# Two changes to the scan pairs of a fused SSD and MLP kernel: B and C turned by VectorE in pairs 2 to 4, and the half form in pairs 4 and 5

## The chip, the core and the metric

The kernel runs on one core of a Trainium2 chip. TensorE is called PE, VectorE DVE, ScalarE ACT, GpSimd POOL; SP only issues DMAs. The time is that of one execution on the device, in microseconds, and the figure of a kernel is the median of its runs. The profile is that of one execution more, with its own span from first to last instruction.

## What is computed

The reference takes a Mamba-2 scan in chunks and puts its result through a two-layer MLP. For batch 4, 8 heads, 768 tokens, head size 32 and state size 16:

```python
log_a = np.log(np.clip(a, 1e-06, 1.0))
# for each chunk c of 32 tokens
cum = np.cumsum(la, axis=-1)
L = np.exp(cum[:, :, :, None] - cum[:, :, None, :]) * causal
M = np.einsum('bhin,bhjn->bhij', Cc, Bc) * L
y = np.einsum('bhij,bhjd->bhid', M, xc) + einsum(Cc, state) * exp(cum)
state = exp(sum(la)) * state + sum_j Bx_j * exp(cum[-1] - cum_j)
# then, over 3072 tokens of width 256
h = x @ w_in                                  # 256 x 2048, float64 weights
g = np.maximum(h, 0) + alpha * np.minimum(h, 0)
out = g @ w_out                               # 2048 x 256
```

The chunk length is free, since the scan gives the same result for any.

## The kernel before

**Pairs and groups.** The 3072 tokens are cut into 24 chunks of 128. Two chunks make a pair (12 pairs, 3 for each batch), two pairs a group of 512 tokens (6 groups). A pair of the scan leaves its result, transposed, in xT, and a group's xT is the moving operand of the MLP. Pairs 0 and 1 are made by `first_two` (L821) in chunks of 64. Pairs 2 and 3 make up group 1 and are run while group 0 goes through the plain MLP, pairs 4 and 5 (group 2) while group 1 goes through the MLP in a form of seven products instead of eight (`quad`, L1229), and so on.

**A pair (`pair`, L581)** is a generator, and `ssm(gp)` takes it one stage further. For pairs 4 and up ("fine") the stages are: the products B'x into a state (L629, or L618 in the half form), the new state (L642, DVE) and its masked copy (L645, POOL); the decays, as four scans over rows of `a` (`scan_half`, L554: DVE reads `abc` and a pattern of ones, `ident_p`, from PSUM); the spread C (`cz`, L679, ACT) and decayed C (`cd`, L682, POOL); the gram products of B and C (L742, or L731 in the half form); their product with the decays (L753, DVE); and the output products (L797 and L805, or L779 and L787), copied to xT by ACT (L817 or L815).

**The half form** applies from pair HALF = 6. A chunk of 128 is then held as two blocks of 64 tokens in the upper and the lower half of the partitions, one chunk in each half. Of the 128 x 128 decay matrix of a head only the causal 128 + 64 columns of the two blocks are made (SQ = 192 columns for the two chunks of a head, in place of 256), so that scans take 192 columns for a head, the gram products 128 and 64. It needs B and x loaded in blocks of 64 tokens (`load_tokens`, L139), rows of `a` with the last 64 columns repeated (`scratch["z", 1]`, written by `rows_out`, L472), the decay products in a matching order (`prt[1]`, L512), a changed lower half of `ident_p` (`halve_identity`, L421), and shifted copies of the decayed C and of the state (`moved`, L685, two ACT and two POOL copies).

**B and C.** Each pair has B by tokens (`nat[:, 0]`, rows of 64 bytes), for the state products. For the gram products B and C are wanted by channels (`bc`). Pairs 2, 3 and 4 load C in the same way (`load_bc`, L188), turn both with four PE transposes (L669) and copy the result from PSUM with ACT (L672). Pairs 5 and up (`turned`) load B and C a second time in rows of 512 bytes, eight tokens to a row (L213 to L217, four DMAs), and DVE turns them in blocks of 32 x 32 (`turn_bc`, L571).

**Weights.** w_in and w_out come as 64-bit floats in 16 pieces of 512 KB and are turned into 32-bit ones by ACT (L273, L283 or L286), POOL (L278), DVE (L296, L308) and POOL (L330). Up to six pieces are in flight.

**What sets the order.** Each engine runs the instructions in the order in which the program lists them, and waits where one needs a result of another; the order is written out by hand. In the loop over f = 4 to 15 (L1454) a step is `hidden(0, f)` on PE, a stage of pair 2 (f up to 10) and of pair 3 (from f = 9), some conversions, and `output(f - 4)`. `load_pair(3)` is issued at f = 5, `load_pair(4)` at f = 10, `bns[3]` and `bns[4]` (L521, POOL) at f = 8 and f = 14. After the loop come the token sums of group 1 (`token_sums`, L1176, POOL) and four stages of pair 4. Then `after(j)` (L1509) places the stages of later pairs between the products of a quad. All loads but a few at the start are issued by SP, in program order, and SP holds an issue back until the eighth DMA before it has landed.

Of the kernel before, what the change touches and what calls it, by code (L numbers as in the profile page):

```python
# [9 lines left out]
F32 = mybir.dt.float32  # L10
# [12 lines left out]
def kernel(  # L23
# [25 lines left out]
    nc = tc.nc  # L49
# [5 lines left out]
    N = B.shape[-1]  # L55
# [21 lines left out]
    WQ = 256  # L77
    HQ = Q // 2
    SQ = Q + HQ
    HALF = NP // 2  # L80
    assert H * N == P and HD == d_model and KC == 2 and R == CPB == 6
    assert NCH % GC == 0 and GT == 512 and NF % 8 == 0 and d_model <= WQ

# [65 lines left out]
    def load_spread(gp, b, c):  # L149

        for w, t in enumerate(loads["p", gp][1] if gp >= HALF else ()):
            rows = scratch["z", b // 2].rearrange("(b h c) t -> b c h t", b=2, h=H)
            for k in range(2):
                nc.sync.dma_start(
                    out=t[HQ * k : HQ * (k + 1), : 4 * SQ].rearrange("p (h t) -> p h t", h=4),
                    in_=rows[b % 2, c + k, 4 * w : 4 * w + 4].unsqueeze(0)
                    .to_broadcast([HQ, 4, SQ]))
        for k, t in enumerate(loads["p", gp][1] if gp < HALF else ()):
            rows = scratch["z", b // 2].rearrange("(b h c) t -> b c h t", b=2, h=H)[b % 2, c + k]
            nc.sync.dma_start(out=t.rearrange("p (h t) -> p h t", h=H),  # L160
                              in_=rows.unsqueeze(0).to_broadcast([P, H, Q]))
            yield
# [7 lines left out]
    def load_pair(gp, decays=True, parted=False):  # L170


        b, c = divmod(2 * gp, CPB)
        turned = gp > GC
        nat = ldx.tile([P, 3, 2, H * N], F32, name="nat")
        xt = ldx.tile([P, 2, HD], F32, name="xt")

        ap = ldx.tile([P, 2 * Q], F32, name="ap")
        if gp == 0:
            load_a(ap, b, c)  # L180
        elif gp > NB:
            load_products(gp, ap)
        if gp == 0:
            load_rows(0, nc.scalar)
        abc = []
        if gp >= HALF:
            load_tokens(nat[:, 0], B[b], c * Q)
        def load_bc(k):  # L188
            ts = slice((c + k) * Q, (c + k + 1) * Q)
            for i, src in enumerate((B,) if turned else (B, C)):  # L190
                eng = nc.scalar if gp == 0 and i else nc.sync
                eng.dma_start(out=nat[:, i, k].rearrange("p (h n) -> p h n", h=H),  # L192
                              in_=src[b, :, ts, :].rearrange("h p n -> p h n"))

        def load_x(k):
            ts = slice((c + k) * Q, (c + k + 1) * Q)
            nc.sync.dma_start(out=xt[:, k].rearrange("p (h d) -> p h d", h=H),  # L197
                              in_=x[b, :, ts, :].rearrange("h p d -> p h d"))

        for k in range((1 if parted else 2) if gp < HALF else 0):  # L200
            load_bc(k)
            if gp >= NB:
                load_x(k)
        for k in range(2 if gp < NB else 0):
            load_x(k)
        if gp == 0:
            nc.scalar.dma_start(out=al_n, in_=moe_alpha.rearrange("(k p) -> k p", p=P))
            loads["a", 1] = prep.tile([P, 2 * Q], F32, name="a1")
            load_a(loads["a", 1], b, c + 2)
        for i, src in enumerate((B, C) if turned else ()):  # L210


            for e in range(2):  # L213
                first = src[b, e : e + 1, c * Q : (c + 2) * Q, :]
                nc.sync.dma_start(out=nat[:, 1 + e, i],
                                  in_=bass.AP(tensor=first.tensor, offset=first.offset,
                                              ap=[[2 * S * N, P // 32], [8 * N, 32], [1, 8 * N]]))  # L217
        for k in range(2 if gp >= NB else 0):
            abc.append(lda.tile([P, H * Q], F32, name="abc"))
        loads["p", gp] = nat, abc, xt, ap  # L220
        if gp >= HALF:
            load_tokens(xt, x[b], c * Q)
        if decays:
            for part in load_spread(gp, b, c):
                pass
        return lambda: load_bc(1), lambda: load_x(1)

    def load_second():

# [190 lines left out]

    def halve_identity():  # L421

        for s in range(2):
            nc.scalar.copy(
                out=ident_p[0][HQ:].rearrange("p (a s t) -> p s a t", a=2, s=2)[:, s],
                in_=ident[HQ:, HQ * (1 - s) : HQ * (2 - s)].unsqueeze(1).to_broadcast([HQ, 2, HQ]))
# [45 lines left out]
    def rows_out(i):  # L472


        if i == 0:
            scratch["z", 0] = dr.tile([RW, Q], F32, name="z0")
            nc.sync.dma_start(out=scratch["z", 0], in_=held.pop("z"))
            return
        d0 = held.pop(i)[:, :SQ]
        rpf = prep.tile([RW, Q], F32, name="rpf")  # L480
        nc.vector.tensor_tensor_scan(out=rpf, data0=d0[:, :Q], data1=zeros[:RW], initial=1.0,
                                     op0=ALU.mult, op1=ALU.add)
        nc.vector.memset(d0[:, :1], 0.0)
        for key, t in (("z", d0), ("pf", rpf)):
            scratch[key, i] = dr.tile([RW, t.shape[1]], F32, name=f"{key}{i}")
            nc.sync.dma_start(out=scratch[key, i], in_=t)

    def rows_short(r):

# [31 lines left out]
    def pair_loads(gp):  # L521

        b, c = divmod(2 * gp, CPB)
        nat, abc, xt, ap = loads["p", gp]

        bn = work.tile([P, 2, H * N], F32, name="bn")
        i, bi = divmod(b, 2)
        if gp >= HALF:
            pj = prt[i].rearrange("p (j b m h) -> p j b m h", j=2, b=2, h=H)[:, :, bi, c // 2]
        else:  # L530
            pj = (prt[i if gp >= NB else "short"]
                  .rearrange("p (b h c) -> p b c h", b=2, h=H)[:, bi, c : c + 2])
        nc.gpsimd.tensor_tensor(
            out=bn.rearrange("p k (h n) -> p k h n", h=H),
            in0=nat[:, 0].rearrange("p k (h n) -> p k h n", h=H),
            in1=pj.unsqueeze(3).to_broadcast([P, 2, H, N]), op=ALU.mult)
        return bn
# [16 lines left out]
    def scan_half(dec, abc, k, w):  # L554
# [10 lines left out]
        for i in range(2):  # L565
# [2 lines left out]
                                         data1=ident_p[0], initial=0.0, op0=ALU.mult,  # L568
                                         op1=ALU.add)

    def turn_bc(gp):  # L571

        bcs[gp] = work.tile([P, 4, Q], F32, name="bc")
        nc.vector.transpose(
            bcs[gp].rearrange("p (i k) t -> p i (k t)", i=2)
            .rearrange("p i (c b) -> p i b c", b=8),
            loads["p", gp][0][:, 1:].rearrange("p e i (b n) -> p (i b) e n", n=N))
        decs[gp] = work.tile([P, 2, H, Q], F32, name="dec")
        scan_half(decs[gp], loads["p", gp][1], 0, 0)

    def pair(gp):  # L581
# [24 lines left out]

        shifted = one.tile([P, 2, P], F32, name="shifted") if half else None

        def added_halves(banks):


            dps = [t[:, : 4 * D].rearrange("p (k m) -> p k m", k=2) for t in banks]
            for j in range(2):
                for r in range(4):
                    rs, hs = slice(32 * r, 32 * r + 32), slice(2 * r * D, 2 * (r + 1) * D)
                    for k in range(nk):
                        ks = slice(HQ * k, HQ * (k + 1))
                        nc.tensor.matmul(dps[k][rs, k], bn[ks, j, rs], xt[ks, j, hs],  # L618
                                         start=False, stop=j == 1,
                                         tile_position=(HQ * k, 32 * r),  # L620
                                         skip_group_check=True)
            return dps
# [30 lines left out]
        if fine:  # L653
            bn = bns.pop(gp) if gp in bns else pair_loads(gp)
            if half:
                dps = added_halves(beside.pop(gp))
            else:
                dps = added(beside.pop(gp) if gp in beside else ss_tile()[:, : 2 * Q])
            yield
# [3 lines left out]

        bc = bcs.pop(gp, None)
        if bc is None:
            tp = ss_tile()
            for i in range(2):
                for k in range(2):
                    nc.tensor.transpose(tp[:, (2 * i + k) * P : (2 * i + k + 1) * P],  # L669
                                        nat[:, i, k], ident)  # L670
            bc = work.tile([P, 4, Q], F32, name="bc")
            nc.scalar.copy(out=bc.rearrange("p i t -> p (i t)"), in_=tp)  # L672
        bh, ct = bc[:, :2], bc[:, 2:].rearrange("p k t -> p (k t)")
        cz = czp.tile([P, 2, 2, Q], F32, name="cz")
        cd = work.tile([P, 2, Q], F32, name="cd")
# [78 lines left out]
            if i == 1:  # L754
                yield
        if fine and gp + 1 < NP:
            if gp + 1 == HALF:
                halve_identity()
                halved.append(True)
            turn_bc(gp + 1)  # L760
        yield

# [691 lines left out]
    for f in range(FIRST, NF):  # L1454
# [5 lines left out]
        for part in range(2):  # L1460
# [5 lines left out]
            for i in CONVERTED.get((f, part), ()):  # L1466
                if isinstance(i, str):
                    convert_a(*pieces[int(i)])
                else:
                    convert_next(first=False)  # L1470
        if f == 14:
            bns[4] = pair_loads(4)
            rows_clamp(1)
# [1 line left out]
            rows_out(1)  # L1475
        if f == 8:
            bns[3] = pair_loads(3)
        output(f - FIRST)
        if f in in_steps:
            weight_sums(wi, in_sums, 0, in_steps[f])  # L1480
    early[0] = None
    beside[GC] = m5_bank[0][:, : 2 * Q]
    token_sums(1)
    ssm(2 * GC // 2, 4)

# [94 lines left out]
```

## Time and profile before

| | us |
|---|---|
| median of 3 runs (356.65 to 358.07) | 356.97 |
| profiled execution: span from first to last instruction | 355.9 |
| PE busy | 349.3 |
| DVE busy | 235.8 |
| POOL busy | 204.4 |
| ACT busy | 171.8 |

The views give no other time of the profiled execution than its span. A line of a timeline has the start in us from the beginning of the span, the length in us, the engine, the line of the code, the operation, what it writes and reads, the shape and the count; in brackets stands how long the engine was idle before it and what ended that. Matmuls are pipelined, so that the length of a PE group overlaps the next one; the distance from one start to the next is what a group takes of PE. In the chain, a line is start, length and what held the end up at that time.

### The profile page before, as it was taken

The page shows a single profiled execution, that of the slowest core. Times are in us where ns is not written, and L with a number is a line of the kernel's source. Part 1 is how long each engine was busy: PE and PEld are TensorE (multiplying, and loading weights), DVE is VectorE, ACT ScalarE, POOL GpSimd, SP SyncE. Part 2 cuts the span into 40 slices and gives each one's busy share as a digit, 9 for nine tenths or more (in the row PEclk, how much of TensorE's full clock was granted, in tenths as well). Part 3 has the DMA queues.
Part 4 walks back from the last instruction along what each step waited for, and adds up shares of the span by engine and source line. Part 5 has one row for each costly group of instructions (what it writes and reads, how often), then busy time and mean ns, then how long its engine had stood idle before and what let it go on. Part 6 is the DMA issues. An engine that isn't in the chain of part 4 may idle for free.

```text
span 355.9 us, 7778 instructions
## 1 busy us (share of the span) xinstructions
PE 349.3 (98%) x2985; PEld 284.4 (80%) x2985; DVE 235.8 (66%) x482; ACT 171.8 (48%) x391; POOL 204.4 (57%) x228
## 2 busy tenths in 40 slices
PE   8899999999999999999999999999999999999996
PEld 4576665578788888888888888888888888888885
DVE  6876986998748756847747856757856633643363
ACT  3477576535355346345345445345445344443431
POOL 6776568589939855725646626637526535434520
PEclk9999999999999999999999999999999999999999
DMA  7899989607345403503423423422001001001102
GB/s 138 182 202 270 329 174 279 148 17 159 106 83 128 102 3 75 104 2 77 78 57 74 86 51 71 85 55 65 11 2 31 0 2 29 2 1 31 31 0 59
DMA packets 105581, 30.24 MB, mean 85 GB/s; under 512 B 79896, under 2 KB 101448, under 8 KB 105544
## 3 DMA queue, kind: packets, MB, share of 16 engines
q1 hardware_dynamic: 103048, 29.43, 36.3%
q10 hardware_dynamic: 2496, 0.32, 0.6%
q8 instruction: 23, 0.38, 0.5%
q14 instruction: 14, 0.11, 0.1%
HBM read 26.32 MB, written 3.42 MB: 84 GB/s over the span
## 4 chain that ended last, share of the span: by engine, by line
PE 89%; SPq 4%; DMA 3%; DVE 2%; ACT 1%; POOL 1%; issue 0%; DVEq 0%; ACTq 0%
PE bank L1216 33%; PE hp L1241 29%; PE bank L1142 6%; PE ss L1241 6%; PE hp L1095 3%; DMA raw<-in_moe_w_in_dram 2%; SPq L192 2%; PE ss L787 1%; PE ss L731 1%; PE hp L1110 1%; PE bank L1209 1%; PE ss L805 1%; PE ss L779 1%; DMA xt<-in_x_dram 1%; SPq L197 1%; PE ss L742 1%
## 5 line engine op out<-in xcount | busy, mean ns | idle before, releaser
L1298 POOL TENSOR_TENSOR gt<-gt 128x512 f32<-128x512 f32 x58 | 74.2, 1279 | 21.1 <-DVE gt L1226 16.3
L1216 PE MATMUL bank<-gt,w_out 128*128 128x256 f32 x320 | 83.5, 381 | 0.0
L1216 PEld LDWEIGHTS bank<-gt,w_out 128*128 128x128 f32 x320 | 60.1, 190 | 9.2 <-issue 1.0
L1288 POOL TENSOR_TENSOR gt<-gt 128x512 f32<-128x512 f32 x20 | 25.4, 1269 | 62.5 <-DVE gt L1226 49.7
L1226 DVE SCALAR_TENSOR_TENSOR gt<-hp,s_mul,gt 128x256 f32<-128x256 f32 x96 | 42.0, 479 | 29.1 <-ACT gt L1224 26.8
L1224 ACT ACTIVATE gt<-hp,s_alpha 128x256 f32<-128x256 f32 x96 | 40.3, 471 | 34.5 <-PE hp L1241 31.4
L1216 PE MATMUL bank<-gt,ws 128*128 128x256 f32 x224 | 55.9, 379 | 0.0
L1216 PEld LDWEIGHTS bank<-gt,ws 128*128 128x128 f32 x224 | 42.3, 190 | 5.6
L1241 PE MATMUL hp<-xs,w_in 128*128 128x256 f32 x160 | 41.9, 384 | 0.0
L1241 PE MATMUL hp<-xs,ws 128*128 128x256 f32 x160 | 41.1, 380 | 0.0
L1267 DVE TENSOR_TENSOR hp<-hp,u 128x512 f32<-128x512 f32 x20 | 14.0, 700 | 35.2 <-ACT u L1265 35.2
L1241 PEld LDWEIGHTS hp<-xs,ws 128*128 128x128 f32 x160 | 30.3, 190 | 4.3 <-POOL xs L1183 0.2
L1241 PEld LDWEIGHTS hp<-xs,w_in 128*128 128x128 f32 x160 | 29.7, 190 | 4.5
L1142 PE MATMUL bank<-w_out,gt 128*128 128x256 f32 x128 | 31.1, 385 | 0.4 <-POOL w_out L330 0.4
L1142 PEld LDWEIGHTS bank<-w_out,gt 128*128 128x128 f32 x128 | 23.6, 190 | 7.2 <-issue 2.9
L1241 PE MATMUL ss<-xT,w_in 128*128 128x256 f32 x96 | 24.6, 379 | 0.0
L645 POOL TENSOR_TENSOR sm<-state,bmask 128x256 f32<-128x256 f32 (+1 forms) x10 | 6.2, 620 | 29.0 <-DVE state L642 29.0
L1095 PE MATMUL hp<-xT,w_in 128*128 128x512 f32 x48 | 22.8, 596 | 0.0
L561 DVE TENSOR_TENSOR_SCAN dec<-abc,bank 128x192 f32<-128x192 f32 x48 | 22.7, 522 | 0.0
L1256 ACT COPY m<-hp 128x512 f32<-128x512 f32 x8 | 4.7, 586 | 35.7 <-PE hp L1241 35.7
L1265 ACT COPY u<-hp 128x512 f32<-128x512 f32 x20 | 11.7, 585 | 19.4 <-PE hp L1241 19.4
L1226 DVE SCALAR_TENSOR_TENSOR gt<-c,s_mul,gt 128x256 f32<-128x256 f32 x40 | 20.6, 555 | 0.0
(232 smaller groups left out, 608.2 us busy)
## 6 DMA issues: line engine op xcount, KB each, us to landing
abc<-z SPq DMA_DIRECT2D x24, 192.0 KB
raw<-in_moe_w_in_dram SPq DMA_DIRECT2D x8, 512.0 KB
raw<-in_moe_w_out_dram SPq DMA_DIRECT2D x8, 512.0 KB
abc<-z SPq DMA_DIRECT2D x8, 512.0 KB
out_dram<-o_sb SPq DMA_DIRECT2D x32, 64.0 KB
nat<-in_B_dram SPq DMA_DIRECT2D x26, 64.0 KB
xt<-in_x_dram SPq DMA_DIRECT2D x12, 128.0 KB
xt<-in_x_dram SPq DMA_DIRECT2D x24, 64.0 KB
```

Of the source, the lines that this page charges most:

```text
L192: eng.dma_start(out=nat[:, i, k].rearrange("p (h n) -> p h n", h=H), in_=src[b, :, ts, :].rearrange("h p n -> p h n"))
L561: nc.vector.tensor_tensor_scan(out=dv[:, o : o + SQ], data0=abc[k][:, s : s + SQ], data1=ident_p[0][:, :SQ], initial=0.0, op0=ALU.mult, op ...
L1095: nc.tensor.matmul(hp, w_in[:, k, f * P : (f + 1) * P], xts[g][:, k], start=(k == 0), stop=(k == KC - 1))
L1142: nc.tensor.matmul(pos[0][t // 2][:, t % 2], gt[:, t * Q : (t + 1) * Q], w_out[:, f], start=(f == 0 and t % 2 == 0), stop=(f == NF - 1), s ...
L1216: nc.tensor.matmul(ms[g][i][:, h], w, blocks[g, z][n][:, p], start=(q == 0 and h == 0), stop=(q == NQ - 1), skip_group_check=True)
L1224: nc.scalar.mul(o[:, p], h[:, p], s_alpha[:, fs[p]])
L1226: nc.vector.scalar_tensor_tensor(out=o[:, p], in0=h[:, p], scalar=s_mul[:, fs[p]], in1=o[:, p], op0=ALU.mult, op1=ALU.max)
L1241: nc.tensor.matmul(to[:, p], w(2 * z + p), b, start=start and p == 0, stop=True, skip_group_check=True)
L1265: nc.scalar.copy(out=u2, in_=A)
L1267: nc.vector.tensor_tensor(out=Y, in0=Y, in1=u2, op=ALU.add)
L1288: nc.gpsimd.tensor_tensor(out=tc_, in0=g22, in1=g12, op=ALU.subtract)
L1298: eng.tensor_tensor(out=o, in0=x0, in1=x1, op=ALU.subtract)
```

## The change

`turned` now holds from pair 2 on and HALF is 4 in place of 6.

Pairs 2, 3 and 4 no longer load C in rows of 64 bytes; they load B and C a second time in rows of 512 bytes. For pair 2, whose loads are issued in two parts, the four new DMAs are issued with the second part. DVE turns the blocks: for pair 2 and pair 4 at the stage in which PE turned them before, for pair 3 at f = 8, ahead of its first stage. The PE transposes and the ACT copy are gone.

Pairs 4 and 5 take the half form. For that the rows of batches 0 and 1 are written once more with their last 64 columns repeated (`rows_repeated`, POOL and one DMA, at f = 6), the decay products are copied into the order of the half form (`rows_halved`, four ACT copies, at f = 12), and the lower half of `ident_p` is changed at f = 13 in place of the last stage of pair 5. Pair 4's state products go into two banks in place of one, and the first of them starts the accumulation there.

```diff
-    HALF = NP // 2
+    HALF = GC
...
-            rows = scratch["z", b // 2].rearrange("(b h c) t -> b c h t", b=2, h=H)
+            rows = scratch["zs", b // 2].rearrange("(b h c) t -> b c h t", b=2, h=H)
...
-        turned = gp > GC
+        turned = gp >= NB
...
-        for i, src in enumerate((B, C) if turned else ()):
-            for e in range(2):
-                first = src[b, e : e + 1, c * Q : (c + 2) * Q, :]
-                nc.sync.dma_start(out=nat[:, 1 + e, i], in_=bass.AP(...))
+        def load_blocks():
+            for i, src in enumerate((B, C)):
+                for e in range(2):
+                    first = src[b, e : e + 1, c * Q : (c + 2) * Q, :]
+                    nc.sync.dma_start(out=nat[:, 1 + e, i], in_=bass.AP(...))
+        if turned and not parted:
+            load_blocks()
...
-        return lambda: load_bc(1), lambda: load_x(1)
+        return lambda: (load_bc(1), load_blocks()), lambda: load_x(1)
...
     def halve_identity():
+        halved.append(True)
...
+    def rows_repeated():
+        d0 = held.pop(0)
+        nc.gpsimd.tensor_copy(out=d0[:, Q + 1 :], in_=d0[:, HQ + 1 : Q])
+        nc.gpsimd.memset(d0[:, :1], 0.0)
+        scratch["zs", 0] = dr.tile([RW, SQ], F32, name="zs0")
+        nc.sync.dma_start(out=scratch["zs", 0], in_=d0)
+
+    def rows_halved():
+        t = prep.tile([P, RW], F32, name="prth")
+        for v in range(2):
+            for j in range(2):
+                nc.scalar.copy(out=t[HQ * v : HQ * (v + 1)]..., in_=prt[0][HQ * j : HQ * (j + 1)]...)
+        prt["halves"] = t
...
+    def turned_bc(gp):
+        bc = work.tile([P, 4, Q], F32, name="bc")
+        nc.vector.transpose(bc..., loads["p", gp][0][:, 1:].rearrange("p e i (b n) -> p (i b) e n", n=N))
+        return bc
...
-                dps = added_halves(beside.pop(gp))
+                dps = added_halves(beside.pop(gp), gp == HALF)
...
         if bc is None:
-            tp = ss_tile()
-            for i in range(2):
-                for k in range(2):
-                    nc.tensor.transpose(tp[:, (2 * i + k) * P : (2 * i + k + 1) * P],
-                                        nat[:, i, k], ident)
-            bc = work.tile([P, 4, Q], F32, name="bc")
-            nc.scalar.copy(out=bc.rearrange("p i t -> p (i t)"), in_=tp)
+            bc = turned_bc(gp)
...
         if fine and gp + 1 < NP:
-            if gp + 1 == HALF:
-                halve_identity()
-                halved.append(True)
             turn_bc(gp + 1)
...
+        if f == 6:
+            rows_repeated()
+        if f == 12:
+            rows_halved()
+        if f == 13:
+            halve_identity()
...
         if f == 8:
             bns[3] = pair_loads(3)
+            bcs[3] = turned_bc(3)
...
-    beside[GC] = m5_bank[0][:, : 2 * Q]
+    beside[GC] = [m5_bank[0][:, : 2 * Q], ss_tile()[:, 2 * Q :]]
```

More of the change, by code (lines that the diff above doesn't have):

```diff
@@ L209, in load_pair @@
             load_a(loads["a", 1], b, c + 2)
-        for i, src in enumerate((B, C) if turned else ()):
-            for e in range(2):
-                first = src[b, e : e + 1, c * Q : (c + 2) * Q, :]
-                nc.sync.dma_start(out=nat[:, 1 + e, i],
-                                  in_=bass.AP(tensor=first.tensor, offset=first.offset,
-                                              ap=[[2 * S * N, P // 32], [8 * N, 32], [1, 8 * N]]))
+        def load_blocks():
+            for i, src in enumerate((B, C)):
+                for e in range(2):
+                    first = src[b, e : e + 1, c * Q : (c + 2) * Q, :]
+                    nc.sync.dma_start(out=nat[:, 1 + e, i],
+                                      in_=bass.AP(tensor=first.tensor, offset=first.offset,
+                                                  ap=[[2 * S * N, P // 32], [8 * N, 32], [1, 8 * N]]))
+        if turned and not parted:
+            load_blocks()
         for k in range(2 if gp >= NB else 0):
@@ L483, in rows_out @@
         nc.vector.memset(d0[:, :1], 0.0)
-        for key, t in (("z", d0), ("pf", rpf)):
+        for key, t in (("zs", d0), ("pf", rpf)):
             scratch[key, i] = dr.tile([RW, t.shape[1]], F32, name=f"{key}{i}")
             nc.sync.dma_start(out=scratch[key, i], in_=t)
+    def rows_repeated():
[8 more added lines that the diff above has]
+            for j in range(2):
+                nc.scalar.copy(
+                    out=t[HQ * v : HQ * (v + 1)]
+                    .rearrange("p (j b m h) -> p j b m h", j=2, b=2, h=H)[:, j],
+                    in_=prt[0][HQ * j : HQ * (j + 1)]
+                    .rearrange("p (b h m k) -> p k b m h", b=2, h=H, k=2)[:, v])
+        prt["halves"] = t
     def rows_short(r):
@@ L528, in pair_loads @@
         if gp >= HALF:
-            pj = prt[i].rearrange("p (j b m h) -> p j b m h", j=2, b=2, h=H)[:, :, bi, c // 2]
+            pj = prt[i if i else "halves"].rearrange(
+                "p (j b m h) -> p j b m h", j=2, b=2, h=H)[:, :, bi, c // 2]
         else:
@@ L569, in scan_half, with turn_bc @@
                                          op1=ALU.add)
-    def turn_bc(gp):
-        bcs[gp] = work.tile([P, 4, Q], F32, name="bc")
+    def turned_bc(gp):
+        bc = work.tile([P, 4, Q], F32, name="bc")
         nc.vector.transpose(
-            bcs[gp].rearrange("p (i k) t -> p i (k t)", i=2)
+            bc.rearrange("p (i k) t -> p i (k t)", i=2)
             .rearrange("p i (c b) -> p i b c", b=8),
             loads["p", gp][0][:, 1:].rearrange("p e i (b n) -> p (i b) e n", n=N))
+        return bc
+    def turn_bc(gp):
+        bcs[gp] = turned_bc(gp)
         decs[gp] = work.tile([P, 2, H, Q], F32, name="dec")
@@ L607, in pair, with added_halves @@
         shifted = one.tile([P, 2, P], F32, name="shifted") if half else None
-        def added_halves(banks):
+        def added_halves(banks, fresh=False):
             dps = [t[:, : 4 * D].rearrange("p (k m) -> p k m", k=2) for t in banks]
@@ L618, in added_halves @@
                         nc.tensor.matmul(dps[k][rs, k], bn[ks, j, rs], xt[ks, j, hs],
-                                         start=False, stop=j == 1,
+                                         start=fresh and j == 0, stop=j == 1,
                                          tile_position=(HQ * k, 32 * r),
```

## The prediction, made before the result was known

> **What bounds the kernel now.** I read the busy shares first, then the chain that ended last, then that chain in order of time, and last the timelines of single engines.
>
> ```profile
> PE 349.3 (98%) x2985; PEld 284.4 (80%) x2985; DVE 235.8 (66%) x482; ACT 171.8 (48%) x391; POOL 204.4 (57%) x228
> ...
> PE 89%; SPq 4%; DMA 3%; DVE 2%; ACT 1%; POOL 1%; issue 0%; DVEq 0%; ACTq 0%
> ```
>
> PE is busy in 98% of the span and holds 89% of the chain, at the full granted clock. So time can only come off by taking work from PE, and only where nothing else is due at the same moment. The second point needs the chain in order of time. These are its pieces from 29.8 us (start, length, what):
>
> ```profile
> 29.84 7.45 DMA raw<-in_moe_w_in_dram
> ...
> 38.13 0.83 POOL wt L278
> 38.96 0.02 issue
> 38.98 0.69 DVE wr L308
> 39.67 0.66 DVE gt L1099
> 40.34 2.33 DVE dec L567 x4
> 42.66 0.64 DVE gt L1099
> ...
> 44.52 1.28 POOL w_out L330
> 45.80 0.04 issue
> 45.84 1.99 PE bank L1142 x8
> ```
>
> Here PE waits (0.44 us, by its timeline) for a converted piece of w_out. The conversion goes back over POOL and DVE to a piece of w_in that landed at 37.3. Up to 45.84 the end is set by the weights and not by PE. From there on the chain is all PE, but the other engines run close behind:
>
> ```profile
> 56.84 0.69 DVE L308 SCALAR_TENSOR_TENSOR wr<-wt,wr 128x512 uint32<-128x512 uint32 x1 [3.08 <-POOL wt L278]
> ...
> 68.25 0.75 DVE L1099 SCALAR_TENSOR_TENSOR gt<-hp,s_mul,gt 128x512 f32<-128x512 f32 x1 [0.27 <-ACT gt L1098]
> ```
>
> DVE has no gap between these two rows. POOL has none from 50.22 to 56.8, which is what holds DVE until 56.84; and DVE has none from 38.98 to 50.1, which is what releases POOL at 50.22. After 68.25 it goes on: DVE L308 (70.64), POOL L330 (72.36, 75.26), bn L533, a weight sum L1171, and the first token sum at 78.55 to 79.28. PE takes that sum at 79.35:
>
> ```profile
> 78.48 1.03 PE L1241 MATMUL ss<-xT,w_in 128*128 128x256 f32 x4
> 79.35 1.11 PE L1241 MATMUL hp<-xs,ws 128*128 128x256 f32 x4
> ```
>
> So a second chain over DVE and POOL runs from 38 to 79 us with 0.27 us of play beside PE. After 79.35 PE shows no gap and the others wait for PE (POOL 49.7 us in all for DVE L1226, ACT 31.4 for PE).
>
> **Part 1: the turning of B and C leaves PE.** Each group of four transposes of L669 costs PE the distance from its start to the next group's start:
>
> ```profile
> 51.09 0.66 PE L669 MATMUL ss<-ident,nat 128*128 128x128 f32 x4
> 51.59 1.89 PE L1142 MATMUL bank<-w_out,gt 128*128 128x256 f32 x8
> ```
>
> That is 0.50 us for pair 3; pair 2 gives 29.46 - 29.02 = 0.44, pair 4 78.48 - 77.99 = 0.49; together 1.43. With them go three ACT copies (L672) of 0.59, beside idle time of ACT. DVE gets three block transposes of 1.11 each (L574). For pair 2 that one stands at 31.25, where DVE idled 1.17 us for a landing: covered. For pair 3 it stands at 50.0, and the 3.08 us of idle before 56.84 take it in. For pair 4 it stands at 78.7 ahead of six scans, which shrink by 6 x (664 - 522) ns = 0.85 us, so DVE is 0.3 us later, within the 0.62 it idles before 82.92. If such a cover were gone, 1.11 each would be on the path.
>
> [...]
>
> **Part 2: pairs 4 and 5 in the half form.** The trace has both forms. Gram products, start to next group's start: pair 4 89.89 to 91.12 = 1.23, pair 5 118.47 to 119.55 = 1.08, pair 6 (half) below = 0.84, and again 0.84 for pairs 7 to 10.
>
> ```profile
> 146.11 0.45 PE L731 MATMUL ss<-cz,bc 32*64 32x256 f32 x4
> ...
> 146.95 1.13 PE L1216 MATMUL bank<-gt,w_out 128*128 128x256 f32 x4
> ```
>
> Saved 0.39 + 0.24. Output products with the next pair's state products, from the L1216 group before them to the L1241 group after them: pair 4 96.41 to 99.09 = 2.68 against pair 7, at the same place of its batch, 178.51 to 181.12 = 2.61; pair 5 123.97 to 126.92 = 2.95 against pair 8's 205.57 to 208.28 = 2.71. Saved 0.07 + 0.24. Pair 4's own state products stay (0.36 against 0.38). Sum 0.94, all after 79.35 where PE alone sets the pace. DVE saves 16 x 0.14 on scans and 8 x 0.13 on L753 there, which is worth nothing.
>
> **Part 3: small additions.** Two ACT copies (L690, 0.30 each) and two POOL copies (L692, 0.29) per pair: in pair 4 ACT must wait for cd, which ends on POOL at 85.4, so the next ACT group starts at 86.0 instead of 85.68 and DVE behind it gives it back from gaps of 0.26 and 0.60; PE next needs that PSUM tile in the following quad. The repeated rows on POOL lie near 42 us in a gap of 1.89 (never shown; between L692's 0.29 and L437's 0.64). The halved prt (four copies, 0.69 in L515's row) and the halved identity (0.56) lie in ACT gaps of 2.59 and 1.15. All at nothing; without cover some 0.3 each.
>
> **Part 4: the queue.** For pair 2, SP loses two C issues (0.58 each) and gains four of L215 (0.55 each) ahead of a w_in piece: 1.0 us more issuing. DMA time falls: in 82 to 84 us 2158 small packets kept 16 engines 82.2% busy, 12 ns each; in 84 to 88 us 1343 packets of 512 B 59.9%, 28.5 ns each. 2048 x 12 becomes 512 x 28.5, over 16 engines 1.54 becomes 0.91: 0.6 us less. So the weights may land 0.6 earlier to 1.0 later. I take 0: the issues of 17.19, 19.43 and 22.24 last 1.6 to 2.2 us, so SP is held by the transfers and the two effects meet. For pair 3 the blocks should land near 50, as DVE wants them; a wait of up to 1.6 us is covered. Pair 4's loads go from 2 x 512 to 4 x 192 KB for the decays and have until 76.
>
> **The sum.** All of it, 1.43 + 0.94 = 2.4. But PE's 1.43 lies ahead of 79.35, where the second chain allows 0.27, so I count 0.3: pair 2's saving becomes a longer wait at 45.84, pair 4's a wait for the token sum. 0.94 + 0.3 = 1.2 off the span of 355.9 gives 354.7. The median of the runs (356.97) is 1.1 above that span; the profiled execution has no time of its own in the views, so I carry 1.1: **355.7 us**. Unknown: the weights (-0.6 to +1.0) and the pace of DVE beside POOL (L308 lasts 0.69 to 1.58, bn 0.62 to 1.14: up to 0.9 either way; I take 0, since the same instructions meet).
>
> **Rivals.**
> - The full sum arrives: the weights land 0.6 earlier and the DVE and POOL stretch shortens as its overlaps fall differently. 355.9 - 2.4 + 1.1 = 354.6. For it: fewer packets, three ACT copies less. Against it: POOL L1171 and L1183 ahead of 79.35 stay where they are.
> - Slower: the four block loads of pair 2 hold the weights. Other loads of B and C show issues of 2.16, 3.52 and 3.89 us where the queue is full. One block issue of that kind (3.5) in front of the w_in piece, with the 1.0 above less 0.6 from DMA, delays the landing of 37.3 and so 45.84 by 3.9: 355.7 + 3.9 = 359.6. It decides from a landing 1.2 us late (no gain) and 3 us late (slower by 0.5%). Against it: the block loads of later pairs all issue in 0.53 to 0.66.
> - Nothing: the four block issues delay the landing by their full 1.0 us and DMA gives nothing back, so 45.84 and all behind it come 1.0 later: 355.7 + 1.0 = 356.7.
>
> **How the numbers follow.** Forecast 0.50, full sum 0.25, nothing 0.15, slower 0.10. A difference of 0.5% (1.8 us) is about what a measurement can tell from no change: faster means below 355.2. That is the full sum and a sixth of the forecast's cases (0.33); slower is 0.10; the rest 0.57. The range takes in the full sum (354.6, less the 0.2 by which slots of one kind differ between pairs: 0.84 against 0.83, 2.61 against 2.71) and, above, a landing 1.0 late with half of the 0.9 on DVE (355.7 + 1.5): 354.4 to 357.2. What it leaves out is the slower rival.
>
> **What would show it.** No L669 on PE; grams of pairs 4 and 5 in 0.84; the gap at 45.84 grown from 0.44 toward 0.9; a gap of some 0.4 ahead of the token-sum group near 79; none after it. Wrong: PE without these gaps (then 354.6), DVE waiting for a nat landing ahead of its transposes, or a gap after 80 us.

## The result, and the profile after

The changed kernel takes 359.45 us (median of 5 runs, 358.14 to 360.35) where the kernel before takes 356.72 (5 runs, 355.82 to 358.07): 1.0069 times as long, 95% interval 1.0051 to 1.0087. The interval lies clear of 1, so it is slower, and the prediction (355.7, range 354.4 to 357.2) is wrong in sign. Run again beside its repairs it took 360.22, 1.0109 times (1.0087 to 1.0130). The profiled execution has a span of 357.7 against 355.9, at a granted clock of 1.000 in both.

The page after, its first and fourth part:

```profile
PE 350.1 (98%) x3093; PEld 284.4 (80%) x3093; DVE 235.7 (66%) x485; ACT 172.5 (48%) x396; POOL 205.2 (57%) x234
...
PE 76%; DVE 7%; POOL 5%; SPq 4%; DMA 4%; issue 2%; ACT 2%; POOLq 0%; DVEq 0%; ACTq 0%
```

PE's busy share did not move, yet PE holds 76% of the chain where it held 89%: DVE and POOL now stand in it. The busy share hid the loss, the chain shows it. In order of time it says where:

```profile
44.65 1.28 POOL w_out L333
45.93 0.04 issue
45.97 1.99 PE bank L1163 x8
...
53.39 1.21 issue
54.60 0.72 POOL ws L1192
55.33 1.03 issue
56.35 1.47 POOL w_in L333
57.82 0.07 issue
57.90 0.62 POOL wt L281
58.52 0.02 issue
58.54 0.69 DVE wr L311
```

Up to the w_out group nothing changed (45.97 against 45.84). From 53 to 59 us POOL and DVE carry the end, and before them stands "issue": the engine waited for something that the view does not name. The timelines name it. Here are DVE's and POOL's, first of the kernel before, then of the changed one:

```profile
50.31 0.75 DVE L1099 SCALAR_TENSOR_TENSOR gt<-hp,s_mul,gt 128x512 f32<-128x512 f32 x1 [0.24 <-ACT gt L1098]
50.98 0.80 DVE L296 TENSOR_SCALAR wr<-raw 128x512 uint32<-128x512 uint32 x1
```

```profile
52.33 1.14 POOL L533 TENSOR_TENSOR bn<-nat,prt 128x256 f32<-128x256 f32 x1
53.44 1.44 POOL L1171 TENSOR_TENSOR ws<-w_in 128x512 f32<-128x512 f32 x1
```

```profile
52.49 1.12 DVE L599 STREAM_TRANSPOSE bc<-nat 128x512 f32<-128x512 f32 x1 [2.29 <-DMA nat<-in_C_dram]
53.45 0.69 DVE L1120 SCALAR_TENSOR_TENSOR gt<-hp,s_mul,gt 128x512 f32<-128x512 f32 x1
54.06 0.41 DVE L299 TENSOR_SCALAR wr<-raw 128x512 uint32<-128x512 uint32 x1
54.57 0.69 DVE L311 SCALAR_TENSOR_TENSOR wr<-wt,wr 128x512 uint32<-128x512 uint32 x1
55.18 1.50 DVE L299 TENSOR_SCALAR wr<-raw 128x512 uint32<-128x512 uint32 x1
58.54 0.69 DVE L311 SCALAR_TENSOR_TENSOR wr<-wt,wr 128x512 uint32<-128x512 uint32 x1 [1.86 <-POOL wt L281]
```

```profile
52.40 0.64 POOL L558 TENSOR_TENSOR bn<-nat,prt 128x256 f32<-128x256 f32 x1
54.60 1.79 POOL L1192 TENSOR_TENSOR ws<-w_in 128x512 f32<-128x512 f32 x1 [1.56 <-issue]
56.35 1.46 POOL L333 TENSOR_TENSOR w_in<-wr,wg 128x512 uint32<-128x512 uint32 x1
```

DVE runs in program order. Pair 3's turn stands at the head of its queue and waits 2.29 us for the last block of C. Behind it come the PReLU (the activation of the MLP) and the sign L299 (a step in the conversion of a weight piece), 3.1 us later than before (53.45 and 54.06 against 50.31 and 50.98). By the code POOL's weight sum takes its output buffer from the same six that hold the raw weight pieces, and the sign reads such a piece. The view names no releaser, but the sum starts 0.13 to 0.14 us after the sign ends (54.47), here and in each of the four other profiles in which the turn waited over 1.2 us. Before, it started at 53.44, when POOL's own bn had ended. So POOL is 1.16 late. It loses 0.35 more while the sum runs beside the next sign (1.75 from its start to the next one, against 1.40) and 0.20 on the conversion behind it (1.55 against 1.35), and hands 1.70 back to DVE (58.54 against 56.84). PE meets this in the grams of pair 3 (62.31 to 64.17, so 1.86, where it was 62.57 to 63.65, so 1.08) and in a wait for the PReLU; from DVE and POOL it comes down to the token sum, 1.7 late:

```profile
67.22 1.98 PE L1116 MATMUL hp<-xT,w_in 128*128 128x512 f32 x4 [1.05 <-DVE gt L1120]
...
81.01 1.13 PE L1262 MATMUL hp<-xs,ws 128*128 128x256 f32 x4 [0.17 <-POOL xs L1204]
```

The last of these stood at 79.35. So 1.66 us are lost up to here, although 1.43 of work had left PE. From the token sum to the first group after pair 5's output products the kernel before takes 126.92 - 79.35 = 47.57, the changed one 128.77 - 81.01 = 47.76. That group in the two kernels:

```profile
126.92 1.13 PE L1241 MATMUL hp<-xs,w_in 128*128 128x256 f32 x4
```

```profile
128.77 1.13 PE L1262 MATMUL hp<-xs,w_in 128*128 128x256 f32 x4
```

The 0.94 that should come off there is missing too; in its place 0.19 is lost. Behind it the two spans have the same left (229.0 and 228.9), so 1.66 and 0.19 are the whole difference of the profiled executions. The trace has the reason for the second in pair 5. First ACT in the kernel before, then ACT, POOL and PE in the changed one:

```profile
113.69 0.84 ACT L1224 ACTIVATE gt<-hp,s_alpha 128x256 f32<-128x256 f32 x2 [1.01 <-issue]
```

```profile
116.07 0.60 ACT L714 COPY shifted<-cd 64x128 f32<-64x128 f32 x2 [1.90 <-POOL cd L706]
116.69 0.84 ACT L1245 ACTIVATE gt<-hp,s_alpha 128x256 f32<-128x256 f32 x2
```

```profile
112.73 1.27 POOL L1192 TENSOR_TENSOR ws<-w_out 128x512 f32<-128x512 f32 x1
114.08 1.27 POOL L1192 TENSOR_TENSOR ws<-ws,w_out 128x512 f32<-128x512 f32 x1
115.31 0.73 POOL L706 TENSOR_TENSOR cd<-bc,ap 128x256 f32<-128x256 f32 x1
```

```profile
119.98 0.45 PE L755 MATMUL ss<-cz,bc 32*64 32x256 f32 x4
...
120.85 0.43 PE L755 MATMUL hp<-cz,bc 32*64 32x256 f32 x2 [0.20 <-DVE gt L1247]
...
121.64 1.13 PE L1237 MATMUL bank<-gt,w_out 128*128 128x256 f32 x4
```

POOL makes cd behind two weight sums. Before, only the output products read cd, which come later. Now ACT's copy of it stands ahead of ACT's part of the PReLU (L1245) and waits 1.90; that part comes 3.29 ahead of the grams (116.69 to 119.98) and no longer 4.78 (113.69 to 118.47), DVE's halves of the PReLU after them, and the PSUM tile that they free is the one that the gram products take third. The grams last 121.64 - 119.98 = 1.66 where the half form takes 0.84. In pair 4 ACT waits 0.72 and they last 92.69 - 91.57 = 1.12.

### The profile page after: what moved, and what is told of

Read it like the earlier page. It is cut to its first block, busy times and chain, and to the rows that moved or that the text cites. A ratio compares the mean times of both kernels' runs of the same rounds, so it can differ in the third digit from the quotient of the medians.

```text
span 357.7 us, 8031 instructions
## 1 busy us (share of the span) xinstructions
PE 350.1 (98%) x3093; PEld 284.4 (80%) x3093; DVE 235.7 (66%) x485; ACT 172.5 (48%) x396; POOL 205.2 (57%) x234
## 4 chain that ended last, share of the span: by engine, by line
PE 76%; DVE 7%; POOL 5%; SPq 4%; DMA 4%; issue 2%; ACT 2%; POOLq 0%; DVEq 0%; ACTq 0%
PE bank L1237 31%; PE hp L1262 27%; PE ss L1262 5%; DMA raw<-in_moe_w_in_dram 4%; PE bank L1163 3%; SPq L192 2%; DVE dec L592 2%; PE ss L808 2%; PE ss L755 1%; DVE wr L311 1%; PE ss L800 1%; DVE gt L1120 1%; POOL gt L1319 1%; PE hp L341 1%; PE hp L1116 1%
## 5 line engine op out<-in xcount | busy, mean ns | idle before, releaser
L1245 ACT ACTIVATE gt<-hp,s_alpha 128x256 f32<-128x256 f32 x96 | 40.3, 471 | 32.1 <-PE hp L1262 31.0
L586 DVE TENSOR_TENSOR_SCAN dec<-abc,bank 128x192 f32<-128x192 f32 x64 | 30.2, 523 | 0.0
L1296 DVE TENSOR_TENSOR c<-hp,m 128x512 f32<-128x512 f32 x20 | 13.8, 692 | 10.6 <-PE hp L1262 10.6
```

The source lines that it names most:

```text
L586: nc.vector.tensor_tensor_scan(out=dv[:, o : o + SQ], data0=abc[k][:, s : s + SQ], data1=ident_p[0][:, :SQ], initial=0.0, op0=ALU.mult, op ...
L1245: nc.scalar.mul(o[:, p], h[:, p], s_alpha[:, fs[p]])
L1296: nc.vector.tensor_tensor(out=c22, in0=A, in1=m5, op=ALU.add)
```

## The experiments

**Theory A**: (1) pair 3's turn, queued on DVE ahead of work that POOL waits for, passes on its wait for the DMA; (2) in pairs 4 and 5 the copies of moved C, queued on ACT behind a late cd, cost the grams what the half form saves. **Rival B**: the turn's own 1.1 us on DVE costs the time wherever it stands. **Rivals D and E** for (2): the copies' length, or the half form itself.

Every kernel starts from the changed kernel, and its line numbers are up to 12 higher. Two stretches of PE are compared, since the executions differ in where the first begins (44.3 to 46.2 us): I from the w_out group of 45.84 to the first product that reads a token sum, II from there to the first group after pair 5's output products. "Wait" is that of pair 3's turn for its blocks; the ratio is to the kernel before beside it.

| kernel | wait | I | II | ratio (95%) |
|---|---|---|---|---|
| before | | 33.51 | 47.57 | 1 |
| changed | 2.29 | 35.04 | 47.76 | 1.0069 (1.0051 to 1.0087) |
| changed, again | 3.76 | 36.48 | 47.79 | 1.0109 (1.0087 to 1.0130) |
| late turn | 1.55 | 34.67 | 47.75 | 1.0071 (1.0053 to 1.0090) |
| early blocks | 0 | 33.69 | 47.74 | 1.0019 (1.0005 to 1.0033) |
| turn only | 1.57 | 34.34 | 47.60 | 1.0041 (1.0022 to 1.0060) |
| half form only | | 33.39 | 47.75 | 1.0014 (0.9997 to 1.0030) |
| turn in the gap | 0 | 33.47 | 47.77 | 1.0014 (0.9995 to 1.0033) |
| turn behind | 0 | 34.35 | 47.77 | 1.0037 (1.0019 to 1.0054) |
| cd early, early blocks | 0.44 | 33.45 | 47.40 | 1.0011 (0.9996 to 1.0026) |
| copies late, early blocks | 1.23 | 33.99 | 46.79 | 0.9986 (0.9967 to 1.0005) |
| gap and copies late | 0 | 33.49 | 46.78 | 0.9990 (0.9974 to 1.0005) |
| half form, copies late | | 33.39 | 46.79 | 0.9978 (0.9969 to 0.9987) |
| gap and copies late, sums first | 0 | 33.15 | 46.68 | 0.9970 (0.9954 to 0.9986) |

**Late turn.**

```diff
         if f == 8:
             bns[3] = pair_loads(3)
-            bcs[3] = turned_bc(3)
```

> The changed kernel, except that VectorE turns pair 3's B and C at that pair's own first stage (iteration 9 of the loop over f) and no longer at iteration 8, at the head of its queue. Theory A (the turn stood at the head of VectorE's queue and waited 2.29 us for the last C block; the PReLU, sign and shift work behind it came 3.1 us late, GpSimd's weight sum behind that 1.56): the wait is gone or below 0.5, the first token sum is back near 79.4 (81.0 in the changed kernel), and the time falls by about 1.6 us against the changed kernel, so 1.0 above the kernel before, 0 to 1.5. Rival B (the token sum is late because VectorE has 1.1 us more work per pair or because the 512-byte rows delay the weights, wherever the turn stands): token sum still near 81, time within 0.4 us of the changed kernel, 2.5 above before.

Measured: the wait is still 1.55, and the time is that of the changed kernel. A's numbers (wait gone, 1.6 us back) did not come; the time of the changed kernel is what B expected. But the edit moved the turn behind one PReLU only; the sign that POOL needs still stood behind it, and the turn still waited. So the run does not tell A from B; it shows that the place was not late enough.

**Early blocks.**

```diff
         for k in range((1 if parted else 2) if gp < HALF else 0):
             load_bc(k)
-            if gp >= NB:
+            if gp >= NB and gp != 3:
                 load_x(k)
...
         if turned and not parted:
             load_blocks()
+        if gp == 3:
+            load_x(0)
+            load_x(1)
```

> The changed kernel, except that pair 3's four block loads of B and C are issued ahead of its two x loads (same loads, other order on SyncE's queue); the turn stays at the head of VectorE's queue in iteration 8. Theory A (the wait for the landing is the cost, not the turn): blocks land 2 us or more earlier, VectorE waits under 0.5 us at the turn, the token sum is near 79.4, the time about 1.6 us below the changed kernel, 0 to 1.5 above before. Rival B (VectorE's added 1.1 us per pair is the cost): the token sum stays within 0.5 of 81 although the wait is gone. Rival C (x then lands too late and the state products of pair 3 wait): a TensorE or GpSimd wait for a landing of xt or nat in 50 to 60 us and no gain.

Measured: the issue of the last block ends at 45.1, 0.8 behind the w_out group, and not at 47.9, 1.9 behind it, and DVE finds the blocks there:

```profile
48.49 1.15 DVE L602 STREAM_TRANSPOSE bc<-nat 128x512 f32<-128x512 f32 x1
49.49 0.67 DVE L1123 SCALAR_TENSOR_TENSOR gt<-hp,s_mul,gt 128x512 f32<-128x512 f32 x1
...
55.56 0.69 DVE L314 SCALAR_TENSOR_TENSOR wr<-wt,wr 128x512 uint32<-128x512 uint32 x1 [3.08 <-POOL wt L284]
```

The same turn at the same place costs next to nothing once its data are there: DVE idles the same 3.08 for POOL as in the kernel before, and stretch I is 33.69, 0.18 above before. A holds, B and C fall. In two later profiles with this order of loads the wait was 0.44 and 1.23, so it is no safe repair.

**Turn only**: HALF back to 6, with the three `rows_` and `halve_` calls of the loop taken out.

> The first part of the change alone: pairs 2 to 4 are turned by VectorE as in the changed kernel, pairs 4 and 5 stay in the full form of the kernel before. Theory A for the second part (in pairs 4 and 5 the two ScalarE copies of moved C wait for cd at the head of ScalarE's queue, 0.72 and 1.90 us, so a PSUM tile comes free late and the grams last 1.12 and 1.66 instead of 0.84; the half form brings nothing, -0.2 us): the time is within 0.5 us of the changed kernel, 1.5 to 2.7 above before, pair 4 and 5 grams at 1.23 and 1.08. The prediction as written (half form worth 0.94): 0.9 above the changed kernel, 3.4 above before.

**Half form only**: pairs 2 and 3 loaded and turned by PE as before.

> The second part of the change: pairs 4 and 5 in the half form, pair 4 turned by VectorE (the half form loads need that), pairs 2 and 3 loaded and turned by TensorE as before. Theory A: the token sum comes near 79.4 again, and behind it the grams of pairs 4 and 5 still last about 1.1 and 1.6 us with waits of ScalarE for cd of 0.7 and 1.9, so the time is that of the kernel before within 0.5 us. The prediction as written (half form worth 0.94 behind the token sum): 0.9 below the kernel before. Rival B (the halves' small additions delay the token sum by themselves): token sum near 81, 1.5 or more above before.

Measured: the part without the half form loses in stretch I (34.34, wait 1.57) and nothing to speak of in II (47.60). The part without the early turn loses nothing in I and 0.18 in II, with ACT's waits for cd unchanged and grams of 1.11 and 1.67. For the turn alone A expected 1.5 to 2.7 above before; the medians lie 1.4 apart, with a wait of 1.57 where the changed kernel had 2.29. The half form alone is 0.35 above, within A's 0.5 and not 0.9 below as the prediction has it. Neither part gives what the prediction says.

**Turn in the gap.**

```diff
+                    if i == 11:
+                        sign(*pieces[11])
+                        bcs[3] = turned_bc(3)
                     convert_next(first=False)
```

(and the line at f = 8 gone, pair 3's first stage at the end of f = 9). **Turn behind** has the turn after the whole loop over conversions at f = 9.

> The changed kernel, with the loads as it has them, but pair 3's turn stands later on VectorE: behind the PReLU and the sign of piece 11 and ahead of its shift, which in the kernel before waits 3.08 us for GpSimd (56.84). Theory A (the cost is what is queued behind the turn while it waits for its blocks, since GpSimd's weight sum and shift wait for those instructions): no wait for the landing, the wait for GpSimd is again 2 us or more after the turn is taken in, the stretch from the w_out group at 45.97 to the first token sum goes from 35.0 us back to 33.2 to 33.7, and the time is that of the kernel with early blocks (0.6 above before), within 0.6. Rival B (a turn of 1.1 us on VectorE costs its length wherever it stands): the stretch is 34.3 or more, the time 1.5 above before.

> As the kernel with the turn in the gap, but one place later: behind the shift that waits for GpSimd, at the head of the stretch where VectorE has no gap up to 68 us. Theory A (only a place with a gap is free): the stretch from the w_out group to the first token sum is 0.8 to 1.2 us longer than with the turn in the gap, 34.2 to 34.7. Rival C (VectorE's length never sets the end in this stretch, GpSimd alone does): the same as in the gap, within 0.3.

DVE in the kernel with the turn in the gap, then with the turn behind:

```profile
52.05 0.87 DVE L299 TENSOR_SCALAR wr<-raw 128x512 uint32<-128x512 uint32 x1
52.84 1.11 DVE L599 STREAM_TRANSPOSE bc<-nat 128x512 f32<-128x512 f32 x1
56.01 0.69 DVE L311 SCALAR_TENSOR_TENSOR wr<-wt,wr 128x512 uint32<-128x512 uint32 x1 [2.06 <-POOL wt L281]
```

```profile
56.46 0.69 DVE L311 SCALAR_TENSOR_TENSOR wr<-wt,wr 128x512 uint32<-128x512 uint32 x1 [3.08 <-POOL wt L281]
57.07 1.10 DVE L599 STREAM_TRANSPOSE bc<-nat 128x512 f32<-128x512 f32 x1
```

In the gap the turn comes out of the idle time, 3.08 to 2.06, and stretch I is 33.47. One instruction later it costs 0.88 (34.35). Both came as A expects; rivals B and C fall.

**cd early** and **copies late**, both on the kernel with early blocks.

```diff
+        if half and gp < 6:
+            c_decayed()
         yield
```

```diff
         gram = products_bc()
+        if half and gp < 6:
+            moved()
```

(each with the call at its old place left out for these two pairs).

> The kernel with early blocks (pair 3's blocks ahead of its x), and in pairs 4 and 5 GpSimd makes cd (C times the decay products) right after the pair's states and no longer after its last scans, so that it stands ahead of the late weight sums. Theory A for the second part (ScalarE's copies of moved C wait for cd and hold the PReLU copies behind them, so that VectorE frees the third PSUM tile of the grams late): ScalarE's waits for cd (0.72 and 1.90 us) are gone, the grams of pairs 4 and 5 last 0.84 to 0.9 instead of 1.10 and 1.66, and the time is about 1.0 us below the kernel with early blocks: 0.4 below before. Rival D (the two copies' own 0.6 us on ScalarE are enough to make the tile late): grams shorten by under half, gain under 0.5. Rival E (the half form of pairs 4 and 5 is slow by itself): no change in the grams.

> The kernel with early blocks, and in pairs 4 and 5 the two ScalarE and two GpSimd copies of the moved halves are issued behind the gram products and no longer behind the last scans; cd stays where it is. Theory A: ScalarE has no wait for cd and no copy ahead of the PReLU, so the grams of pairs 4 and 5 last 0.84 to 0.95 and the time is about 1.0 us below the kernel with early blocks. Rival D (the copies' length counts, not the wait): here too they are gone from that place, so this one gains and the kernel with early cd gains only half of it. Rival E (the half form is slow by itself): grams stay at 1.10 and 1.66.

Measured: with the copies late the grams of pair 5 take 119.87 - 119.03 = 0.84, those of pair 4 0.99, and stretch II is 46.79; the prediction's 47.57 - 0.94 would be 46.63. With cd early ACT's waits are gone and pair 4's grams take 0.99 too, but II is only 47.40 and pair 5's grams still take 1.44, not the 0.9 that A expected. That looks like rival D and is not: measured from the token sum ACT's part of the PReLU starts at the same moment in both kernels (112.66 - 78.67 and 114.25 - 80.21, 34.0 each), though one has the moved copies ahead of it. What differs is DVE, here with cd early and then with the copies late:

```profile
L1253 DVE SCALAR_TENSOR_TENSOR gt<-c,s_mul,gt 128x256 f32<-128x256 f32 x2 | 2.9, 1502 | 0.0
L1253 DVE SCALAR_TENSOR_TENSOR gt<-hp,s_mul,gt 128x256 f32<-128x256 f32 x2 | 0.9, 474 | 0.0
```

```profile
L1252 DVE SCALAR_TENSOR_TENSOR gt<-c,s_mul,gt 128x256 f32<-128x256 f32 x2 | 2.1, 1073 | 0.0
L1252 DVE SCALAR_TENSOR_TENSOR gt<-hp,s_mul,gt 128x256 f32<-128x256 f32 x2 | 0.9, 474 | 0.0
```

The last column but one is the mean in ns of one. The PReLU whose operands both lie in SBUF takes 1502 ns with cd early and 1073 with the copies late; the one that reads PSUM takes 474 in both. By the timelines POOL's last two weight sums run from 35.7 to 38.4 us after the token sum in the first kernel, beside nearly all of the two with operands in SBUF (35.7 to 38.6), and 0.8 earlier in the second. So of the 0.97 that the copies cost, 0.36 was the wait and 0.61 came back in pair 5 in the longer PReLU. That it is longer because DVE and POOL run side by side is read from the timelines; no run moved the sums alone. E falls too.

**The changed kernel again.**

> The changed kernel once more, unaltered, for a second profile and for runs beside those of its repairs. Theory A (VectorE's wait at the head of its queue for pair 3's last C block sets the loss): time 2 to 3 us above before; the stretch from the w_out group near 45 to the first token sum is 33.1 plus what the turn waits for beyond about 0.3, so between 34.2 and 35.2; the grams of pairs 4 and 5 at 1.1 and 1.66 again. Rival F (the profile shown was a poor draw and the typical execution has no such wait): wait under 0.5, stretch under 33.8, time within 1.0 of before.

```profile
53.03 1.11 DVE L599 STREAM_TRANSPOSE bc<-nat 128x512 f32<-128x512 f32 x1 [3.76 <-DMA nat<-in_C_dram]
```

The wait is longer, 3.76, stretch I as much longer, 36.48, more than the upper end expected (35.2), because the wait is: by the expectation's own rule it would be 36.6. The time, 3.8 above before, is above A's 2 to 3 as well. F falls.

**Both repairs, the half form repaired alone, and the token sums first.** The first joins the turn in the gap and the late copies, the second the half form only and the late copies; the third adds to the first:

```diff
-        if f in in_steps:
+        if f in in_steps and f < 14:
             weight_sums(wi, in_sums, 0, in_steps[f])
...
     token_sums(1)
+    weight_sums(wi, in_sums, 0, 3)
```

> Both repairs: pair 3's turn in VectorE's gap (as measured: 0.6 above before) and the copies of the moved halves of pairs 4 and 5 behind their gram products (as measured: 1.0 less). The whole change is otherwise in it. Theory A: the two add, 0.4 below before (355.6 to 356.6 where before is 356.4), grams of 0.99 and 0.84, stretch to the token sum 33.2 to 33.7. If the gains overlap: within 0.3 of before.

> Pairs 2 and 3 loaded and turned by TensorE as before, pairs 4 and 5 in the half form (pair 4 turned by VectorE), the copies of the moved halves behind the gram products. Theory A: the half form alone measured 0.35 above before; with the grams repaired (0.78 more off behind the token sum) 0.4 below before, and equal to the kernel with both repairs within 0.5, since TensorE's 0.94 for the transposes of pairs 2 and 3 lies ahead of the token sum, where VectorE and GpSimd set the time. The prediction's full-sum rival (those 0.94 come off): this one 0.9 slower than the kernel with both repairs.

> Both repairs, and GpSimd makes the four token sums ahead of the last part of the first weight sums (1.39 us) and no longer behind it. Theory A (a chain over VectorE and GpSimd, whose last piece is this one, holds the first token sum): TensorE's wait of 0.16 for xs goes and VectorE's PReLU is next, so the time is 0.1 to 0.3 below the kernel with both repairs. Rival (GpSimd's queue is the whole chain): up to 0.8 below it. Rival (the weight sum then comes late for the products that read it): a TensorE wait for w_in behind 81 us and a loss of up to 1.0.

Measured 355.82, 355.57 and 355.43, with 356.40 before. The repairs add as expected, though the first can't be told from the kernel before by its interval; the last two are faster than the kernel before by 0.2% and 0.3%, by intervals that lie just below 1. The first and the second have one stretch II (46.78, 46.79) and stretches I of 33.49 and 33.39, though the second leaves the 0.44 + 0.50 of transposes of pairs 2 and 3 on PE. So the rival by which these 0.94 come off falls. With the token sums first PE's wait for xs is gone, stretch I is 0.34 shorter and the time 0.4 lower, a little more than the 0.1 to 0.3 expected; the wait for w_in that its rival feared does not come, II is 46.68:

```profile
78.40 1.13 PE L1264 MATMUL ss<-xT,w_in 128*128 128x256 f32 x4
79.37 1.03 PE L1264 MATMUL hp<-xs,ws 128*128 128x256 f32 x4
```

## Why the prediction was wrong

**The step that failed** is in its part 4: "For pair 3 the blocks should land near 50, as DVE wants them; a wait of up to 1.6 us is covered." Both halves fell. The issue of the last block ended at 47.9 and DVE waited for it until 52.49, and until 53.03 the second time. And of the wait only some 0.75 us was covered, not 1.6. The kernels with the turn at f = 8 show the size ("sum late" is the start of POOL's first weight sum, counted from the w_out group, against the 7.60 of before):

| kernel | wait | sum late | stretch I above before |
|---|---|---|---|
| copies late, early blocks | 1.23 | -0.03 | 0.48 |
| turn only | 1.57 | 0.30 | 0.83 |
| changed | 2.29 | 1.03 | 1.53 |
| changed, again | 3.76 | 2.47 | 2.97 |

The sum is late by the wait less 1.26 to 1.29, and the stretch grows by 0.5 more than that. The 1.26 can be read in the rows: the sign of 50.98 ends at 51.78 and the sum starts at 53.44, a play of 1.66; to it come the 0.24 that DVE idled ahead of its PReLU and 0.45 by which PReLU and sign run shorter behind the turn; off go 0.96 for the turn (52.49 to 53.45) and 0.13 from the sign's end to the sum. The 0.5 is what sum and conversion take longer, with the next sign beside the sum: 1.75 + 1.55 from start to start in all four, where before it was 1.40 + 1.35. With a wait of 0.44 (cd early) nothing is lost.

The 3.08 us of idle that were to take the wait in end with POOL, and the prediction counted POOL as held by its own work ("POOL has none from 50.22 to 56.8"). But POOL's sum of 53.44 also needs DVE's sign of 50.98. The rows were in the profile of before. The prediction asked what DVE idles for, and not what that releaser waits for in its turn. It did name the sign by which this would show: "DVE waiting for a nat landing ahead of its transposes".

**The second chain** was read rightly. PE's 1.43 brought nothing ahead of the token sum: stretch I is 33.47 with the turn in the gap and 33.39 with pairs 2 and 3 on PE, against 33.51. Even the 0.3 counted is not seen, and PE's gap ahead of the w_out group, which was to grow to 0.9, is 0.44 in both kernels. What was missed is that the chain has no play in the other direction either: what makes DVE or POOL later there makes the token sum later.

**The half form's 0.94** was the right size for PE alone (0.78 arrives once the copies are late) and in the changed kernel it is -0.19. The mis-sized term is part 3's "All at nothing": for pair 4 the copies were worked through, for pair 5, where ACT waits 1.90 for cd, not. They cost 47.76 - 46.79 = 0.97 together, 0.82 of it in pair 5's grams (1.66 and 0.84) and 0.13 in pair 4's (1.12 and 0.99). Of the 0.16 still missing, 0.15 is pair 4's grams, 0.99 where 0.84 was expected; the reason for that stays open.

**Right or harmless**: the transposes are off PE; the rows repeated and halved and the halved identity lie in gaps, and nothing waits for them. Pair 2's part of the queue did not delay the w_out group (45.97 against 45.84, PE's gap 0.44 in both); whether it does so by some tenths can't be told, since that group starts between 44.3 and 46.2 in the other profiles. The turn's own length did not decide either: its 1.1 us cost 0.18 with its blocks landed and nothing in the gap. The slower rival had the right cause, block loads that arrive late, but at pair 2 and through SP's queue and the weights; it came at pair 3 and through DVE's queue.

**The base of the sum** was off by some 0.6: the time of an execution is 1.7 above its span (359.45 and 357.7 after), not 1.1, so the execution profiled before was itself one of the longer ones, at some 357.6. That leaves an open end: the medians lie 2.7 apart and the profiled spans 1.8, which is all that the two profiles account for. Whether the other 0.9 is a later start of the w_out group or a longer wait of other executions, no trace decides.

## What to carry to other kernels

Idle time covers an added wait only as far as what ends it does not depend on the same queue (here some 0.75 of 3.08 us): follow the releaser back until it leaves the engine, and take the smallest play on the way. An instruction that waits for a transfer belongs behind the work that others wait for and ahead of the engine's own next wait; here one place further on DVE made 0.9 us. Of an operation added in several places, each place needs its own look at what stands ahead of its operand on the producing engine.

## What the runs showed of the hardware

- The last of pair 3's four block loads landed 3.8 to 5.5 us after the end of its issue, by the end of DVE's wait in six profiles (waits of 0.44 to 3.76).
- DVE and POOL took longer in some places where they ran side by side. The sign L299, with one input, took 0.41 us while POOL idled (54.06) and 1.50 beside POOL's sum (55.18); that sum took 1.79, and another 1.28 a few us later (62.81), most of it beside DVE's scans. The PReLU with two operands in SBUF took 837 (changed kernel), 1073 and 1502 ns at the same place of pair 5, as POOL's weight sums ran beside the two of them for 0.9, 1.8 and 2.6 us; the one that reads PSUM took 472 to 474 there, in the changed kernel with POOL's sums beside it (117.61 to 118.49). No run shows why some are slower and others not.
- In the kernel before SP's issue of 37.30 began 0.72 us after the end of the one ahead of it, and 0.01 after the transfer issued eight before it (29.84) had landed (37.29). Its issues of B and C that lasted 3.52, 3.89 and 2.16 us (9.40, 37.30, 44.31) had a DMA busy share of 0.92, 1.04 and 0.48 beside them, by the packets that started meanwhile; that the queue was full there no view shows.
